# The last wq slabs of a backward pass: requested earlier, into store buffers, and turned in place

## The chip, the cores and the metric

The kernel runs on one core of a Trainium2 chip. The metric is the device time of one execution in microseconds (us), the median of several runs. A profile of one further execution gives the trace; its span is the time from the first to the last instruction of the core.

The engines are named as the profile names them: PE (TensorE, matrix products and transposes), PEld (its weight loads), DVE (VectorE), ACT (ScalarE), POOL (GpSimd, which here copies a little and issues the stores) and SP (SyncE, which here only issues the loads). The loads of SP form the DMA queue q1, the stores of POOL the queue q0. Both are served by the same 16 DMA engines.

## The reference

A decoder step for one token: attention over a cache, a feed-forward layer with squared ReLU, the same attention again and the same feed-forward layer again, with the same weights both times, and the gradients of everything with respect to the inputs (`jax.vjp`). D = 1024, 32 query heads of 128 in 4 groups, a cache of 4 x 65536 x 128 for K and for V, F = 3584, all in bf16.

```python
def _A_ref(x, k_cache, v_cache, wq, wo):
    q = (x @ wq).reshape(B, Sq, Hq, Dh).transpose(0, 2, 1, 3)
    k = jnp.repeat(k_cache, rep, axis=1)
    v = jnp.repeat(v_cache, rep, axis=1)
    scores = jnp.einsum("bhqd,bhkd->bhqk", q, k) * (Dh ** -0.5)
    p = _softmax(scores, axis=-1)
    o = jnp.einsum("bhqk,bhkd->bhqd", p, v)
    return o.transpose(0, 2, 1, 3).reshape(B, Sq, Hq * Dh) @ wo
...
x = x + _A_ref(_layernorm(x), A_k_cache, A_v_cache, A_wq, A_wo)
x = x + _B_ref(_layernorm(x), B_w1, B_b1, B_w2, B_b2)
x = x + _A_ref(_layernorm(x), A_k_cache, A_v_cache, A_wq, A_wo)
x = x + _B_ref(_layernorm(x), B_w1, B_b1, B_w2, B_b2)
```

The outputs are the result and the gradients of x, K, V, wq, wo, w1, b1, w2 and b2.

## The kernel before

**Four passes over the cache.** The K and V caches are read once in each of four passes: the first attention forward, the second forward, the second backward (its dq), and in the last pass (`attn_bwd4`, L1297) dq of the first attention and the K and V gradients of both. Between the passes stand the feed-forward layers. In the code L1 is the first attention layer, L3 the second.

**The arena.** K and V blocks, weight slabs and staged outputs share one buffer in SBUF, `arena`, cut into 20 slots of 128 x 4096 bf16 (1 MB each). A `Slot` (L314) takes a free one, `free` gives it back. In the last pass the slots are of two kinds: those in the set `RING` are meant for stores, the others for loads. `take_one` (L292) gives a caller with `fill=True` the slot of the ring that has been free longest, and any other caller one from outside the ring. When the last group's turn comes, the ring has 11 slots. The kernel only says which slot is used; the waits follow from it: a load into a slot waits until the last reader or the last store of that slot is done.

**The last pass.** It runs over 256 items of 8 columns of 128 positions each, group after group (64 items each), the last group being group 0. Each item goes through the stages in L1484: `vT` turns the V block (8 transposes on PE, L1353, and a copy out of PSUM), `vS` multiplies it with dO, `eT` and `xT` turn the probabilities and their gradients, `dV8` and `dK8` make the output blocks (L1434, copies L161 on ACT or L164 on DVE, store L1440), and `k8` (L1465) multiplies the K block with the gradients for dq. The stages of one item lie some items apart. K and V come in halves of 32 columns, 1 MB each, and one half serves four items. `kv8` (L351) asks for a half at its first use in the program's order, but SP issues requests as soon as the slot is free, so it runs ahead of the engines. SP issues strictly in its own order: a request that waits for its slot holds all behind it. The pass is not ordered by hand; a scheduler arranges each engine's instructions, SP's among them.

**Copies.** `evac` (L150) copies a PSUM tile out, on ACT or DVE, whichever has the smaller planned load; in the last pass bf16 tiles lean to DVE.

**Background work.** `bg` steps other work between the items: outer products for the weight gradients (`g_outer`, `g_outer_wide`, staged in ring slots; stores L1552, L1573), and for each group but the last `g_dn` (L998), which adds that group's part of the gradient `dn1` from two wq slabs by row products on DVE (L595) and sums on ACT (L584).

**The last group's part of dn1.** It needs dq of group 0, known only after the last `k8`, so it is the end of the kernel: `on4` (L1997), called after the last `fold_dq` (L1202). To make it short, wq's slabs for group 0 are loaded and turned ahead. There are two slabs of four row blocks of 128 x 1024 each (L458, 1 MB a slab, runs of 2 KB in DRAM). The class `Rows` (L609) turns them: `tra` (L684) does 8 transposes (L688) and one copy for each of 8 rows of 128 x 1024, `back` (L715) does 8 products with dq for each row (L722), and the sum goes to `dn_finish`. Where `inplace` is not set, `tra` writes the turned row to a view of two further slots (`s_wt`, L619). Then come the layer norm's backward, dx0, and the last outer product `g_outer_last` (L1515).

**When.** The list `end` at L2024 gives functions to be called n items before the end of the pipeline (L871): at 20 the two slabs are requested, into load slots; at 10 `fill4` takes the two `s_wt` slots and turns all eight rows at once, drains the background work and begins `g_outer_last`.

Of the kernel before, what the change touches and what calls it, by code (L numbers as in the profile page):

```python
# [20 lines left out]
def kernel(  # L21
# [31 lines left out]
    R = HQ // G  # L53
    F = B_w1.shape[1]
    DC, FC = D // P, F // P
# [84 lines left out]
    load = {"act": 0.0, "dve": 0.0, "pe": 0.0}  # L140
# [4 lines left out]
    def add_load(act=0.0, dve=0.0, pe=0.0):  # L145
        load["act"] += act
        load["dve"] += dve
        load["pe"] += pe

    def evac(out, in_, kind="bf"):  # L150
        n = 1
        for d in in_.shape[1:]:
            n *= d
        ca = 0.17 + n * 0.00083
        cd = 0.13 + n * (0.00105 if kind == "f32" else 0.00054)

        if PS["pass4"] and kind == "bf":
            ca += 1.5
        if kind == "kta" or kind != "kt" and load["act"] + ca <= load["dve"] + cd:
            load["act"] += 0.17 + n * 0.00083  # L160
            nc.scalar.copy(out=out, in_=in_)  # L161
        else:
            load["dve"] += cd
            nc.vector.tensor_copy(out=out, in_=in_)  # L164
# [119 lines left out]
    def take_pair():  # L284
        both = [(max(FREE[i], FREE[i + 1]), i) for i in range(0, NG, 2) if i in FREE and i + 1 in FREE]
        if not both:
            return None
        i = min(both)[1]
        del FREE[i], FREE[i + 1]
        return i  # L290
# [20 lines left out]
    def odd_one():  # L311
        return any((i ^ 1) not in FREE and t <= NOW["step"] - 16 for i, t in FREE.items())

    class Slot:  # L314
        def __init__(self, name, fill=False, at=None, both=False, load=False):
            self.i = take_one(fill, load) if at is None else at
            self.n = 2 if both else 1
            self.users, self.over = 0, False
            self.t = wide(self.i) if both else GRAN[self.i]
            BUSY.update(range(self.i, self.i + self.n))  # L320
# [87 lines left out]
    B4_LAG = DK_LAG + J // 8  # L408
# [26 lines left out]
    def rows_of(W):  # L435
        return W.rearrange("(kc p) n -> p kc n", p=P)
# [1 line left out]
    def f_rows_of(W):  # L438
        return W.rearrange("(s p j) n -> p s j n", p=P, j=4)

    def slabs(name, load, nk, kper, ncols, ahead=1, flat=False):
        pend = deque()
        ks = deque(range(0, nk, kper))

        def fetch():
            k = ks.popleft()
            i = None
            if ks and flat and NOW["wide"] and not odd_one():
                i = take_pair()
            if i is None:  # L450
                kn = min(kper, nk - k)
                sl = Slot(name)
            else:
                kn = min(2 * kper, nk - k)
                ks.popleft()
                sl = Slot(name, at=i, both=True)
            v = sl.t[:, 0:kn * ncols].rearrange("p (k n) -> p k n", n=ncols)
            nc.sync.dma_start(out=v, in_=load(k, kn))  # L458
            pend.append((k, kn, sl, v))

        def gen():
            while ks or pend:
                while ks and len(pend) < ahead:
                    fetch()
                k, kn, sl, v = pend.popleft()
                for kk in range(kn):
                    NOW["slab"] = sl
                    yield k + kk, v[:, kk, :]
                sl.over = True
                if not sl.users:  # L470
                    sl.free()
        g = gen()
        g_fetch = [fetch for _ in range(ahead)]
        return g, g_fetch

    def prefetch(pair):

        g, fs = pair
        for f in fs:
            f()  # L480
        return g

    def wq_slabs(g, ahead=1):
        v = rows_of(A_wq)
        return slabs("s_wq", lambda k, kn: v[:, k:k + kn, g * 1024:(g + 1) * 1024], DC, 4, 1024, ahead, True)

    def wo_slabs(g, ahead=1):
        v = rows_of(A_wo)
# [120 lines left out]
    class Rows:  # L609
        def __init__(self, pool=None, bufs=NWT):  # L610
            self.pool, self.bufs = pool, bufs
            self.views = deque()
            self.n = 0
            self.made = 0
            self.parts = 0
            if pool is None:

                for _ in range(2):
                    t = Slot("s_wt").t[:, :].rearrange("p (v a b) -> p v a b", v=4, a=8)  # L619
                    self.views.extend(t[:, v, :, :] for v in range(4))  # L620
                self.bufs = 8
            self.queue = deque()
            self.jobs = deque()
            self.feed = None
# [59 lines left out]
        def tra(self, job, kc, slab, q, kind="bf"):  # L684
            k0, w = job["pieces"][q]
            pt = self.ps_wt()
            for i in range(w):
                nc.tensor.transpose(pt[:, i, :], job["cols"](slab, k0 + i), ident_b[:, :])  # L688
            sl = NOW["slab"]
            if job["inplace"]:  # L690
                wt = slab[:, k0 * P:(k0 + w) * P].rearrange("p (a b) -> p a b", b=P)
            elif self.views:
                wt = self.views.popleft()
            else:
                self.made += 1
                if self.made % 2:
                    wt = ktpool.tile([P, 8, P], BF, name="kt", tag="kt")
                else:
                    wt = self.pool.tile([P, 8, P], BF, name="wt", tag="wt", bufs=4)
            evac(wt[:, 0:w, :], pt[:, 0:w, :], kind)  # L700
            add_load(pe=w * 0.1)
            self.queue.append((job, kc, q, wt, sl))
            if job["inplace"]:
                sl.users += 1
            else:
                self.parts += 1
# [59 lines left out]
        def run(self):  # L766
            self.fill()
            first = self.queue[0][0] if self.queue else None
            while first is not None and first["inplace"] and self.queue and self.queue[0][0] is first:
                self.back()  # L770
            self.fill()
            while self.queue:
                self.back()
                self.fill()
# [140 lines left out]
    def gsl(g):  # L915
        return slice(g * R, (g + 1) * R)
# [73 lines left out]
    def dn_finish(dn, first):  # L990
        def fin(y):
            if first:
                nc.vector.tensor_copy(out=dn[:], in_=y)
            else:
                nc.vector.tensor_tensor(out=dn[:], in0=dn[:], in1=y, op=ALU.add)
        return fin

    def g_dn(L, dn, g, first):  # L998
        yield from g_rowdots(wq_slabs(g)[0], DC, L["dqT"][:, gsl(g)], R, dn_finish(dn, first), "%s_dn%d" % (L["name"], g))
# [594 lines left out]
    L1, L3 = new_layer("L1", 0), new_layer("L3", 1)  # L1594
# [31 lines left out]
    lastg = [ITEMS[p][-1][0] for p in range(4)]  # L1626
    firstg = [ITEMS[p][0][0] for p in range(4)]
    PRE = {}

    def pre_load(key, pair):  # L1630
        def f():
            PRE[key] = prefetch(pair())
        return f

    gxbc = bcast_vec(gx[:], DC)
    bg = Background()
# [18 lines left out]
    rows = Rows(DENSE["pool"])  # L1655
# [20 lines left out]
    bg = Background()  # L1676
# [86 lines left out]
    rows = Rows(DENSE["pool"])  # L1763
    wo3b = wo_slabs(firstg[2])
    eps4 = root_ready(L3, lastg[1])
    ahead = [0]
# [75 lines left out]
    bg = Background()  # L1842
# [17 lines left out]
    rows = Rows(DENSE["pool"])  # L1860
# [110 lines left out]
    b4 = ExitStack()  # L1971
    bgpool = b4.enter_context(tc.tile_pool(name="bgpool", bufs=1))
    bg = Background()
# [6 lines left out]
    dn1 = vec.tile([P, DC], F32, name="dn1")  # L1980
# [16 lines left out]
    def on4(g):  # L1997
        if g != lastg[3]:
            bg.add(g_dn(L1, dn1, g, g == firstg[3]))
            bg.normal.append(gwq(g))  # L2000
        else:
            next(PRE["gwq"])
            PRE["rows"].run()
            next(PRE["gwq"])
            dxn1 = ln_bwd(dn1[:], L1["n"], L1["rstd"])
            dx0 = tmp.tile([P, DC], F32, name="dx0")
            nc.vector.tensor_tensor(out=dx0[:], in0=dx1[:], in1=dxn1[:], op=ALU.add)
            col_to_dram(dx0, D, out_1.rearrange("a b d -> (a b d)"))
            run(PRE["gwq"])

    def last_v():

        for g, c8 in ITEMS[3][-3 * J // 8::J // 8]:
            kv8("v", g, c8)

    def fill4():
        PRE["rows"] = Rows()
        PRE["rows"].add(PRE["wq4"], DC, R, lambda: L1["dqT"][:, gsl(lastg[3])], dn_finish(dn1, False))
        PRE["rows"].fill()
        bg.drain()  # L2020
        PRE["gwq"] = g_outer_last(bgpool, out_4, [L3["n"], L1["n"]], [L3["dqT"][:, gsl(lastg[3])], L1["dqT"][:, gsl(lastg[3])]],
                                  lastg[3] * 1024)
        next(PRE["gwq"])
    attn_bwd4(3, L1, L3, on4, bg, b4, [(12 + B4_LAG, last_v), (20, pre_load("wq4", lambda: wq_slabs(lastg[3], 2))), (10, fill4)])  # L2024
    b4.close()
    ps4_stack.close()

# [29 lines left out]
```

## Time and profile before

| | us |
|---|---|
| median of 3 runs | 1936.69 (1935.64 to 1938.51) |
| the profiled execution | 1936.17 |
| its span | 1934.3 |
| mean granted clock of PE | 0.92 |
| PE busy, DVE busy, ACT busy in the span | 1576.4, 1172.2, 1043.8 |
| moved by DMA | 787.62 MB, mean 407 GB/s |
| slab requests of group 0 on SP | 1853.8 and 1855.5 |
| its transposes (L688) | 1903.1 to 1911.7 |
| last `fold_dq` (L1202) | 1915.9 |

All times of the trace are counted from the start of the span. An engine's busy time is the sum of its instructions; the time between an instruction and the one before it is its wait, and the profile names what ended it. For a DMA the trace has the issue (by SP or POOL) and the landing. In the lists of groups, a row gives line, engine, operation, what is written and read, the count, then busy us and mean ns of one, then idle time ahead of it. In the timeline a row gives start, duration, the work, its count and in brackets the wait ahead of it. In the DMA view a queue's row gives packets, MB, and the share of the 16 engines' time.

### The profile page before, as it was taken

What the parts mean: (1) busy time and instruction counts of PE and PEld (TensorE: products, weight loads), DVE (VectorE), ACT (ScalarE), POOL (GpSimd) and SP (SyncE); (2) the same over time, 40 slices, a digit from 0 to 9 for tenths busy, and PEclk for the clock granted to TensorE, in tenths of its full rate; (3) what the DMA queues carried; (4) which work ended last, traced back from release to release, by engine and by line L of the source; (5) the groups of instructions that cost most, each with busy time, mean ns of one, the idle gap of its engine ahead of it and who ended that gap; (6) DMA issues with size and microseconds to landing.
All of it is one profiled execution on the core that took longest, in us unless ns stands there. A gap on an engine that the chain in (4) does not pass through costs nothing. (4 is left out here: it accounts for less than half of the span.)

```text
span 1934.3 us, 66768 instructions
## 1 busy us (share of the span) xinstructions
PE 1576.4 (81%) x30099; PEld 1292.1 (67%) x30099; DVE 1172.2 (61%) x2448; ACT 1043.8 (54%) x1619; POOL 142.4 (7%) x325
## 2 busy tenths in 40 slices
PE   6878778678878878978787878888996987787977
PEld 6878777678777878867677875555654554454544
DVE  5645555255555554645464576777876886676766
ACT  3434334245333535446363465766876785576765
POOL 0000000000000000000000002111211211121211
PEclk9989999799999988998999999898988998798997
DMA  9999999999999999999999997999999999899998
GB/s 393 427 427 424 429 428 416 399 420 412 428 425 428 428 422 330 379 425 429 426 420 426 405 348 298 425 420 387 424 424 413 420 425 423 349 423 397 425 422 321
DMA packets 107148, 787.62 MB, mean 407 GB/s; under 512 B 9440, under 2 KB 16622, under 8 KB 42222
## 3 DMA queue, kind: packets, MB, share of 16 engines
q1 hardware_dynamic: 82782, 617.65, 77.3%
q0 software_dynamic: 24080, 165.70, 20.5%
q8 instruction: 235, 3.85, 0.7%
q14 instruction: 51, 0.42, 0.1%
HBM read 617.62 MB, written 165.69 MB: 405 GB/s over the span
## 5 line engine op out<-in xcount | busy, mean ns | idle before, releaser
L164 DVE COPY kt<-ps_tr 128x1024 bf16<-128x1024 bf16 x736 | 505.8, 688 | 427.1 <-PE ps_tr L1030 239.5
L161 ACT CAST arena<-ps_gg 128x1024 bf16<-128x1024 f32 x457 | 444.2, 1011 | 183.2 <-PE ps_gg L1434 132.4
L1030 PE MATMUL ps_tr<-ident_b,arena 128*128 128x128 bf16 x3840 | 308.4, 225 | 48.0 <-DMA arena<-in_A_k_cache_dram 35.3
L161 ACT COPY kt<-ps_tr 128x1024 bf16<-128x1024 bf16 x180 | 188.6, 1054 | 184.5 <-PE ps_tr L1224 107.2
L164 DVE CAST arena<-ps_gg 128x1024 bf16<-128x1024 f32 (+2 forms) x186 | 222.4, 1196 | 80.1 <-PE ps_gg L1434 36.0
L1030 PEld LDWEIGHTS <-arena 128*128 128x128 bf16 x3840 | 231.8, 101 | 56.7 <-DMA arena<-in_A_k_cache_dram 37.8
L1434 PE MATMUL ps_gg<-GG,xt 64*128 64x512 bf16 x1024 | 209.8, 408 | 51.2 <-DVE arena L164 36.7
L1131 PE MATMUL ps_acc<-arena 128*128 128x64 bf16 (+4 forms) x4096 | 204.6, 197 | 46.1 <-DMA arena<-in_A_v_cache_dram 33.7
L1048 PE MATMUL ps_sc<-L_qpad,kt 128*128 128x64 bf16 (+7 forms) x3584 | 182.6, 194 | 23.1 <-issue 11.7
L1353 PE MATMUL ps_tr<-ident_b,arena 128*128 128x128 bf16 x1824 | 178.1, 232 | 28.5 <-DMA arena<-in_A_v_cache_dram 25.7
L1113 ACT ACTIVATE arena<-S_sb,L_negm 128x128 bf16<-128x128 f32 x256 | 165.3, 1006 | 57.2 <-DVE L_negm L1098 43.6
L1224 PE MATMUL ps_tr<-ident_b,arena 128*128 128x128 bf16 x2032 | 161.7, 224 | 40.6 <-DMA arena<-in_A_v_cache_dram 39.1
L1131 PEld LDWEIGHTS <-arena 128*128 128x128 bf16 x4096 | 160.0, 101 | 52.1 <-DMA arena<-in_A_v_cache_dram 37.7
L1353 PEld LDWEIGHTS <-arena 128*128 128x128 bf16 x1824 | 117.6, 103 | 84.7 <-issue 54.2
L1048 PEld LDWEIGHTS <-kt 128*128 128x128 bf16 x3584 | 152.0, 100 | 27.3 <-issue 12.8
L1224 PEld LDWEIGHTS <-arena 128*128 128x128 bf16 x2032 | 122.6, 100 | 46.0 <-DMA arena<-in_A_v_cache_dram 41.7
L1465 PEld LDWEIGHTS <-arena 128*128 128x128 bf16 x2048 | 92.4, 101 | 56.4 <-issue 38.5
L1434 PEld LDWEIGHTS <-xt 64*128 64x128 bf16 x1024 | 64.4, 94 | 97.8 <-issue 60.2
L1113 ACT ACTIVATION_READ_ACCUMULATOR arena<-S_sb,L_negm 128x1 f32 x256 | 128.2, 501 | 0.0
L584 ACT ACTIVATE mv_t<-mv_t 128x1024 bf16<-128x1024 bf16 x96 | 102.0, 1064 | 43.0 <-DVE mv_t L595 42.8
L1278 PE MATMUL ps_acc<-dsT,arena 128*128 128x64 bf16 (+7 forms) x2048 | 102.4, 194 | 12.4 <-DMA arena<-in_A_k_cache_dram 7.2
L1390 PE MATMUL ps_sc<-DOB,kt 128*128 128x64 bf16 (+3 forms) x1824 | 112.3, 197 | 0.1
(319 smaller groups left out, 2104.3 us busy)
## 6 DMA issues: line engine op xcount, KB each, us to landing
arena<-in_A_k_cache_dram SPq DMA_DIRECT2D x82, 2048.0 KB, 21.3
arena<-in_A_v_cache_dram SPq DMA_DIRECT2D x79, 2048.0 KB, 20.1
out_dram<-arena POOLq DMA_DIRECT2D x149, 1024.0 KB, 15.6
arena<-in_A_v_cache_dram SPq DMA_DIRECT2D x84, 1024.0 KB, 13.1
arena<-in_A_k_cache_dram SPq DMA_DIRECT2D x84, 1024.0 KB, 14.6
arena<-in_A_wo_dram SPq DMA_DIRECT2D x22, 1024.0 KB, 14.9
arena<-in_B_w_dram SPq DMA_DIRECT2D x21, 1024.0 KB, 10.0
arena<-in_A_wq_dram SPq DMA_DIRECT2D x18, 1024.0 KB, 13.4
```

Of the source, the lines that this page charges most:

```text
L161: nc.scalar.copy(out=out, in_=in_)
L164: nc.vector.tensor_copy(out=out, in_=in_)
L584: nc.scalar.activation(out=t[:, :], in_=t[:, :], func=ACTF.Copy, accum_out=y[:, kc:kc + 1])
L1030: nc.tensor.transpose(pt[:, i, :], kb8[:, i, :], ident_b[:, :])
L1048: nc.tensor.matmul(state["ps_s"][:, s:s + w, :].rearrange("p a b -> p (a b)"), lhsT=kt[:, i, :], rhs=L["qpad"][:, g, 0:w, :].rearrange("p ...
L1113: nc.scalar.activation(out=E(p, g, c0, SU)[:, :, h], in_=S[:, h, :], func=ACTF.Exp, bias=L["negm"][:, g, su, h:h + 1], scale=SCALE, accum_ ...
L1131: nc.tensor.matmul(ps_o[:, 0:w, :], lhsT=vb8[:, i, :], rhs=E(p, g, c, w), start=(c % SU == 0), stop=(c % SU == SU - 1), skip_group_check=True)
L1224: nc.tensor.transpose(pt[:, i, :], vb8[:, i, :], ident_b[:, :])
L1278: nc.tensor.matmul(ps_dq[:, 0:w, :].rearrange("p a b -> p (a b)"), lhsT=kb8[:, i, :], rhs=dsT[:, s:s + w, :].rearrange("p a b -> p (a b)") ...
L1353: nc.tensor.transpose(pt[:, i, :], vb8[:, i, :], ident_b[:, :])
L1390: nc.tensor.matmul(state["ps_dp"][:, s:s + w, :].rearrange("p a b -> p (a b)"), lhsT=vt[:, i, :], rhs=DOB[:, g, 0:w, :].rearrange("p a b - ...
L1434: nc.tensor.matmul(pg[:, 512 * h:512 * h + 512], lhsT=xt[64 * h:64 * h + 64, j1 // 8 + m, :], rhs=gg[64 * h:64 * h + 64, :, :].rearrange(" ...
```

## The change

The two slabs are requested 48 and 38 items before the end instead of both at 20, and into ring slots (`fill=True` by the new argument `ring`). From item -28 on, every second item turns one row (`last_turn`), in place: the copy goes back into the slab's own slot. The two `s_wt` slots and the code for them go. At item -10 `fill4` no longer turns rows; at the end `on4` runs the same products by `begin` and `back`.

```diff
-    def slabs(name, load, nk, kper, ncols, ahead=1, flat=False):
+    def slabs(name, load, nk, kper, ncols, ahead=1, flat=False, ring=False):
...
-                sl = Slot(name)
+                sl = Slot(name, ring)
...
-    def wq_slabs(g, ahead=1):
+    def wq_slabs(g, ahead=1, ring=False):
         v = rows_of(A_wq)
-        return slabs("s_wq", lambda k, kn: v[:, k:k + kn, g * 1024:(g + 1) * 1024], DC, 4, 1024, ahead, True)
+        return slabs("s_wq", lambda k, kn: v[:, k:k + kn, g * 1024:(g + 1) * 1024], DC, 4, 1024, ahead, True, ring)
...
-            self.views = deque()
...
-            if pool is None:
-
-                for _ in range(2):
-                    t = Slot("s_wt").t[:, :].rearrange("p (v a b) -> p v a b", v=4, a=8)
-                    self.views.extend(t[:, v, :, :] for v in range(4))
-                self.bufs = 8
...
-            elif self.views:
-                wt = self.views.popleft()
...
             next(PRE["gwq"])
-            PRE["rows"].run()
+            last_rows.begin(last_job)
+            while last_rows.queue:
+                last_rows.back()
             next(PRE["gwq"])
...
+    last_wq, last_fetch = wq_slabs(lastg[3], 2, True)
+    last_rows = Rows()
+    last_job = last_rows.job(DC, R, lambda: L1["dqT"][:, gsl(lastg[3])], dn_finish(dn1, False))
+    last_job["inplace"] = True
+
+    def last_turn():
+        kc, slab = next(last_wq)
+        run(last_rows.front(last_job, kc, slab))
+
     def fill4():
-        PRE["rows"] = Rows()
-        PRE["rows"].add(PRE["wq4"], DC, R, lambda: L1["dqT"][:, gsl(lastg[3])], dn_finish(dn1, False))
-        PRE["rows"].fill()
+        next(last_wq, None)
         bg.drain()
...
-    attn_bwd4(3, L1, L3, on4, bg, b4, [(12 + B4_LAG, last_v), (20, pre_load("wq4", lambda: wq_slabs(lastg[3], 2))), (10, fill4)])
+    tail = [(48, last_fetch[0]), (38, last_fetch[1])] + [(28 - 2 * k, last_turn) for k in range(DC)] + [(10, fill4)]
+    attn_bwd4(3, L1, L3, on4, bg, b4, [(12 + B4_LAG, last_v)] + tail)
```

In the built programs the arithmetic is the same, instruction for instruction in kind and number, but for the choice between ACT and DVE for one copy. SP's order differs at these places only: the first slab now stands right behind the second slab of group 1's `g_dn` (requested at 1750.06 in the trace of before) and takes a slot whose last store is the one issued at 1750.58; the V half that was requested at 1754.96 stands two places later, behind the K half of 1756.93 and the V half of 1774.18; the second slab stands between the V half of 1792.36 and the K half of 1801.30 and takes a slot whose last store is the one issued at 1792.92; and the two slabs at 1853.79 and 1855.49 are gone. The 64 transposes of the rows are spread over what was 1847 to 1897.

## Prediction

> **What bounds the kernel now.** I read the slices of the page first, then the windows of the last 160 us, then the waits there, then SP's requests and the landing times of its transfers.
>
> ```profile
> DMA  9999999999999999999999997999999999899998
> HBM read 617.62 MB, written 165.69 MB: 405 GB/s over the span
> ```
>
> The DMA engines are full nearly everywhere, and the change moves no byte more or less. So it can only matter where it opens or closes a gap. This window table shows the end of the last pass (busy us and count of PE, PEld, DVE, ACT, POOL, then granted clock, DMA share, GB/s):
>
> ```profile
> 1875.60:1885.00 9.40, 0.03 (x2) 0.00 (x0) 0.33 (x5) 1.20 (x2) 0.53 (x1) 0.76 1.02 427
> 1885.00:1897.50 12.50, 12.42 (x105) 7.00 (x105) 6.92 (x9) 5.63 (x6) 0.53 (x1) 0.50 0.96 401
> ...
> 1860.00:1872.40 12.40, 12.17 (x169) 7.74 (x169) 10.16 (x18) 10.01 (x12) 2.98 (x5) 1.00 1.03 421
> 1902.00:1916.00 14.00, 12.90 (x200) 9.08 (x199) 11.43 (x19) 11.15 (x13) 1.26 (x2) 1.00 1.00 386
> ```
>
> TensorE is the pacing engine (12.17 of 12.4 us busy) until it stands still at 1875.6. Behind that it runs 12.5 us at clock 0.50. The PE timeline names what it waited for there, and at one earlier place:
>
> ```profile
> 1885.08 0.34 PE L1465 MATMUL ps_acc<-X,arena 128*128 128x64 bf16 x3 [9.45 <-DMA arena<-in_A_k_cache_dram]
> ```
>
> ```profile
> 1804.76 0.23 PE L1353 MATMUL ps_tr<-ident_b,arena 128*128 128x128 bf16 x1 [1.84 <-DMA arena<-in_A_v_cache_dram]
> ```
>
> Both are reads. Which half a request brings, and when TensorE first uses it, I took from the order of the built program laid beside the trace. These are SP's requests ahead of the large wait, and those at the places where the changed program's order puts the two slabs:
>
> ```profile
> 1853.79 2.08 SPq L458 DMA_DIRECT2D arena<-in_A_wq_dram  x2
> 1864.37 1.30 SPq L361 DMA_DIRECT2D arena<-in_A_k_cache_dram  x2
> ```
>
> ```profile
> 1750.06 0.38 SPq L458 DMA_DIRECT2D arena<-in_A_wq_dram  x1
> 1754.96 0.33 SPq L361 DMA_DIRECT2D arena<-in_A_v_cache_dram  x1
> 1756.93 0.33 SPq L361 DMA_DIRECT2D arena<-in_A_k_cache_dram  x1
> ```
>
> ```profile
> 1792.36 0.43 SPq L361 DMA_DIRECT2D arena<-in_A_v_cache_dram  x1
> 1801.30 0.33 SPq L361 DMA_DIRECT2D arena<-in_A_k_cache_dram  x1
> 1801.77 0.40 SPq L361 DMA_DIRECT2D arena<-in_A_v_cache_dram  x1
> ```
>
> Last, what the read queue (q1) gets beside the store queue (q0), in 1757 to 1766 with a wq slab at its head, then in 1795 to 1815 with K and V halves alone:
>
> ```profile
> q0 software_dynamic: 403, 2.92, 77.3%
> q1 hardware_dynamic: 397, 0.85, 24.1%
> ```
>
> ```profile
> q1 hardware_dynamic: 621, 4.53, 53.7%
> q0 software_dynamic: 613, 3.92, 46.9%
> ```
>
> Packets are shared about one for one (397 to 403). A wq row is 2 KB and a store's run 8 KB, so a slab (1.05 MB) takes 1.05/(0.85/9) = 11.1 us to pass, a K or V half 1.05/(4.53/20) = 4.6 us. With stores absent (1768.2 to 1772: 1.49 MB in 3.8 us) a slab takes 2.7 us. The Trainium skill ("DMA: Bandwidth & Descriptors", Queues, rings and completion order) says each engine takes turns between its queues by packets; with one 2 KB row against one 8 KB run that gives q1 a fifth of 424 GB/s, an estimate of 12.4 us for a slab, and would add 1.3 us to the sum.
>
> **Part 1, the slabs leave 1853.8 and 1855.5.** Two slow slabs stood ahead of the K halves there. In the changed order the next K halves stand behind the same TensorE counts, so they are asked for at these times, not at 1864.4 and 1865.3. The K half at 1844.19 landed at 1859.6, so they land near 1864 and 1869, 11 us or more before their use at 1875.6 and some 10 us later. The wait of 9.45 us goes. So does the half clock: 105 instructions at the rate of 1860 to 1872.4 (169 in 12.4) take 7.7 us, not 12.5, a gain of 4.8. Sum -14.2. Bounds: -9.5 (the clock falls for some other wait) to -14.2. Next due are the last two K halves; their buffers come free with the same TensorE counts as the halves at 1864, so they too come 30 us earlier than at 1898.
>
> **Part 2, the 64 transposes and 8 copies.**
>
> ```profile
> L688 PE MATMUL ps_tr<-ident_b,arena 128*128 128x128 bf16 x64 | 5.0, 220 | 0.0
> ```
>
> They leave 1903.1 to 1911.7, where PE is 12.90 of 14 us busy, and go to what is now 1847 to 1897, where it is 12.17 of 12.4. PE paces both, so 5.0 us leave and 5.0 come: 0. Bounds: -5.0 if the waits of the new place hide them, +1.1 (the 14 - 12.90 idle at the old one). The copies (six on DVE at 686 ns, two on ACT at 1015 ns, 6.1 us) find 2.2 us free on each engine in every 12.4: hidden.
>
> **Part 3, buffers.** Two buffers for turned rows are no longer taken at item -10; nothing read into that range waits for them. But stores go round 9 buffers, not 11. 18 large stores in 1802 to 1875 are one per 4.06 us: a buffer comes back after 36.5 us in place of 44.6. A store lands 23.2 us after issue (median there), and filling takes about 10 us (four quarters over four items of 2.5 us). 3 us are left: 0. Bounds 0 to +5.
>
> **Part 4, the first slab.** Its buffer was last emptied by the store issued at 1750.58, which took 17.0 us; SP stands until 1767.6 with everything behind it. Behind it are the K half of 1756.93 (used at 1779.6) and the V halves of 1774.18 and 1754.96, in this order. At 1767.6 the store queue runs empty, so the slab passes in 2.7 us, in the place of the V half; K lands just in time. The V half now comes between the V half of 1774.18 and the K half of 1779.8, and every later read lands a half later: 4.6 us, plus some tenths for the late start: 5. The V half of 1790.68 landed at 1804.7, when PE had waited 1.84 us already, so all of it is new wait. Bounds: 0 (1773 to 1782 moved only 2.61 MB, room for one more half) to 7.
>
> **Part 5, the second slab.** It stands between the requests of 1792.36 and 1801.30 and waits for the store issued at 1792.92, 13.1 us, until 1806.0. The K half behind it needs a buffer that part 4 moves from 1801.3 to 1806.3, so SP loses nothing. Then it takes 11.1 us of the read queue. The V half of 1801.77 landed 21.2 us later, at 1823.0, and its transposes began at 1824.74: 1.7 us to spare. New wait 9.4; but TensorE standing still makes no stores, and the two halves behind the slab go faster as the stores run out (from 4.6 us each toward 2.7): I take 2 off, 7.4. Bounds: 1.0 (2.7 - 1.7) to 9.4. What comes next had 6 us or more to spare and shifts with PE.
>
> **Part 6, the clock.** The wait of 1.84 us was followed by 3.4 us at 0.50 and the one of 9.45 by 12.5. Two new waits of 7 us cost 0.5 to 4.8 each by these; I take 2.5 for both. The Trainium skill ("TensorE: Matmul & The Clock Gate", Why this matters for your kernels) sets the limit at gaps of about 3 us; the wait of 1.84 shows the trace less patient, and by the rule both new waits would still cost.
>
> Sum: -14.2 + 0 + 0 + 5 + 7.4 + 2.5 = +0.7. The profiled execution took 1936.17 us (span 1934.3, 1.9 around it), 0.5 below the median of the runs. 1936.2 + 0.7 = 1936.9, by the median 1937.4: I say **1937.5**. From the last group's dq (1915.9) to the end nothing changes.
>
> **Rivals.**
> - *Faster: the reads are not held.* The room of 1773 to 1782 takes the V half (0) and the second slab meets a nearly empty store queue (1.0 to 3, say 2), with 1 for the clock: -14.2 + 3 = -11.2, 1926. For it: the 290 GB/s there, and stores that thin out as soon as PE waits. Against it: q0 was never empty in 1795 to 1815.
> - *Slower: the second slab at the head of the read queue.* Place: 1816 to 1830, ahead of the K and V halves of 1801.3 and 1801.77. Price: 9.4 in full, part 4 at 7, and half clock as after 1885 for one wait and 2 for the other (6.8): 23.2 - 14.2 = +9.0, 1945. It decides once both waits together, clock included, pass 14.2 us. For it: the V halves asked for at 1774.18, 1790.68 and 1801.77 had 0, 0 and 1.7 us to spare, while the reads of 1843.21 and 1844.19, the last ahead of the slabs' old place, had 31 and 6. Against it: the relief by idle stores.
> - *Store buffers:* the old wait goes, but copies wait for one of 9 buffers: +5, 1942. Against it: 3 us of room, and a shorter store backlog after an early wait.
>
> **Chances.** Forecast 0.40, faster rival 0.25, second slab 0.28, store buffers 0.07. A change under 0.2% (3.9 us) can't be told from none here. The forecast's own range is 1933 to 1942; it gives 0.05 faster, 0.28 same, 0.07 slower. The first rival gives 0.22 faster and 0.03 same, the others 0.03 same and 0.32 slower. Together 0.27, 0.34, 0.39. Range 1928 to 1945.
>
> **What would show it.** In the new profile: no wait of TensorE for K near 1875 to 1890, and clock 1.0 there (part 1); L688 spread before the end (part 2); a wait of L1353 for V of some 7 us near 1803 to 1810 (part 4) and of L1465 or L1353 of some 7 near 1829 to 1837 (part 5), each with half clock behind it; no copy waiting for a store (part 3). I am wrong if the two early waits stay under 8 us together or pass 18, or if a K wait remains at the end.

## The result, and the profile after

The changed kernel takes 1942.16 us, the median of 18 runs (1936.24 to 1946.80). The kernel before, run beside it, takes 1936.83 (18 runs, 1929.03 to 1942.41). The ratio is 1.003, with a 95% interval from 1.0018 to 1.0042: the change costs about 5 us. A later repetition (below) gave 1.0031, from 1.0017 to 1.0044.

The profiled execution of the changed kernel took 1936.24 us and was the fastest of its 18. When TensorE resumes after a long wait for DVE (1773.00 us before, 1769.57 after) it was already 3.4 us ahead. About 1 us of that was there at SP's last request ahead of the places where the orders differ (1750.06 before, 1749.06 after). The rest came while the slab of that request landed, in 20.9 us before and 18.5 after; in the profile of the repetition, with the changed order too, it landed in 21.5, so I take the lead for chance. The change's first own request is made at 1764.31. So I compare the stretches behind that point, not the spans: 161.3 us from there to the end before, 164.8 after, and 167.6 in the profile of the repetition (1771.7 to 1939.3).

First three of the windows that the prediction showed of the kernel before, and one for a new slow stretch; the window table's columns are as explained there.

```profile
1875.60:1885.00 9.40, 8.77 (x130) 5.88 (x128) 6.98 (x14) 7.06 (x9) 1.98 (x4) 1.00 1.01 421
1885.00:1897.50 12.50, 11.98 (x167) 7.88 (x166) 10.61 (x22) 10.00 (x12) 2.12 (x4) 1.00 0.99 412
1827.20:1840.80 13.60, 8.22 (x72) 4.71 (x72) 3.21 (x5) 4.56 (x5) 1.27 (x2) 0.50 1.01 426
1902.00:1916.00 14.00, 11.68 (x193) 7.87 (x190) 10.92 (x24) 9.73 (x12) 1.80 (x3) 1.00 0.64 264
```

The standstill at 1875.6 to 1885 is gone (8.77 of 9.4 us busy, clock 1.00), as part 1 said. In its place stands half clock from 1827.2 to 1840.8. And in 1902 to 1916 TensorE is less busy than before (11.68 us, not 12.90), with the DMA engines at 0.64, not full.

The PE timeline, at its three long waits behind 1800:

```profile
1804.03 0.29 PE L1344 MATMUL ps_tr<-ident_b,arena 128*128 128x128 bf16 x1 [2.61 <-DMA arena<-in_A_v_cache_dram]
...
1828.88 0.23 PE L1456 MATMUL ps_acc<-X,arena 128*128 128x64 bf16 x1 [4.38 <-DMA arena<-in_A_k_cache_dram]
...
1833.84 0.40 PE L1344 MATMUL ps_tr<-ident_b,arena 128*128 128x128 bf16 x2 [3.70 <-DMA arena<-in_A_v_cache_dram]
```

The first is the V half of part 4, the two others are the halves behind the second slab, of part 5. SP's requests in the changed kernel:

```profile
1764.31 0.38 SPq L458 DMA_DIRECT2D arena<-in_A_wq_dram  x1
1764.78 0.46 SPq L361 DMA_DIRECT2D arena<-in_A_k_cache_dram  x1
1770.75 1.14 SPq L361 DMA_DIRECT2D arena<-in_A_v_cache_dram  x2
...
1803.96 0.38 SPq L458 DMA_DIRECT2D arena<-in_A_wq_dram  x1
1804.44 0.61 SPq L361 DMA_DIRECT2D arena<-in_A_k_cache_dram  x1
1805.10 0.48 SPq L361 DMA_DIRECT2D arena<-in_A_v_cache_dram  x1
```

The first slab was held for its buffer until 1764.31 and the second until 1803.96, each with K and V behind it. While the second passes, from 1810 to 1822, the two queues show nearly the shares that part 5 had taken from 1757 to 1766:

```profile
q0 software_dynamic: 498, 3.68, 73.2%
q1 hardware_dynamic: 552, 1.32, 27.8%
```

552 packets to 498, but 1.32 MB to 3.68: the read queue brings 1.32 MB in 12 us. The second slab landed 20.1 us after its request, at 1824.0, and the V half ahead of it at 1812.9: 11.1 us to pass, as part 5 had it.

The 64 transposes of the rows, in the list of groups by tile for 1840 to 1905 (ns min/median/max, then first and last start):

```profile
L681 PE MATMUL ps_tr<-ident_b,arena x64: 219/219/230, 1856.3 to 1898.2; 128*128 128x128 bf16 x64
```

They are spread over 42 us, as the change says. The chain of waits at the end of the pass shows what paces there now:

```profile
1903.08 1.02 ACT arena L161
...
1904.14 0.42 PE ps_gg L1503 x2
...
1904.59 1.02 ACT arena L161
...
1905.65 0.41 PE ps_gg L1425 x2
...
1906.08 1.02 ACT arena L161
...
1907.15 0.42 PE ps_gg L1503 x2
...
1907.59 1.02 ACT arena L161
```

ACT copies a product tile out of PSUM in 1.02 us, TensorE fills the next in 0.42, and so on, some 1.5 us a round: from 1903 to 1909 the chain runs through ACT's copies, and TensorE fits its other products in between. (Left out are pieces of 0.02 to 0.04 us, the time to issue.) So TensorE's own work doesn't set the pace there alone.

Stretch by stretch, in us, with what the prediction's parts give for the same stretch:

| from ... to | before | after | difference | predicted |
|---|---|---|---|---|
| TensorE resumes ... first transpose of the late V half (1804.76, 1804.03) | 31.8 | 34.5 | +2.7 | +5 (part 4) |
| ... first transposes of the V half asked for at 1801.77, in the changed kernel at 1805.10 | 20.0 | 29.8 | +9.8 | +9.9 (parts 5 and 6) |
| ... where TensorE comes to the K half that it waited for before (1875.6, 1890.5) | 50.9 | 56.7 | +5.8 | +5.0 (part 2, the transposes come) |
| ... the end | 58.7 | 43.9 | -14.8 | -19.2 (parts 1 and 2, the transposes leave) |
| sum | 161.3 | 164.8 | +3.5 | +0.7 |

The three costs together came as predicted to within 2 us. What lacks is in the last row: 4.4 us of the gain. The third row holds more than transposes, since half clock goes on to 1840.8; what the transposes alone cost there is read below, from the same stretches of three placings.

### The profile page after: what moved, and what is told of

Its sections match the earlier page's. It is cut to its first block, busy times and chain, and to the rows that moved or that the text cites. A ratio compares the mean times of both kernels' runs of the same rounds, so it can differ in the third digit from the quotient of the medians.

```text
span 1934.4 us, 66781 instructions
## 1 busy us (share of the span) xinstructions
PE 1594.3 (82%) x30099; PEld 1302.7 (67%) x30099; DVE 1171.7 (61%) x2447; ACT 1045.3 (54%) x1620; POOL 142.1 (7%) x325
## 5 line engine op out<-in xcount | busy, mean ns | idle before, releaser
L1425 PE MATMUL ps_gg<-GG,xt 64*128 64x512 bf16 x1024 | 215.4, 417 | 38.2 <-DVE arena L164 23.2
L1425 PEld LDWEIGHTS <-xt 64*128 64x128 bf16 x1024 | 63.5, 94 | 86.0 <-issue 49.3
## 6 DMA issues: line engine op xcount, KB each, us to landing
arena<-in_A_wq_dram SPq DMA_DIRECT2D x18, 1024.0 KB, 13.6
```

Of the source, the lines that this page charges most:

```text
L1425: nc.tensor.matmul(pg[:, 512 * h:512 * h + 512], lhsT=xt[64 * h:64 * h + 64, j1 // 8 + m, :], rhs=gg[64 * h:64 * h + 64, :, :].rearrange(" ...
```

## The experiments

Each was timed beside the kernel before: 1936.51 us in the first group of four, 1936.43 in the second, 1938.28 in the third. So the ratio to it counts; a difference of medians from two groups is rough.

**Turning late.** All eight rows are turned at item -10 as before; the requests and the buffers stay as changed.

```diff
-    tail = [(48, last_fetch[0]), (38, last_fetch[1])] + [(28 - 2 * k, last_turn) for k in range(DC)] + [(10, fill4)]
+    tail = [(48, last_fetch[0]), (38, last_fetch[1])] + [(10, last_turn)] * DC + [(10, fill4)]
```

> Requests as in the changed kernel (48 and 38), all eight rows turned in place at item -10. Theory (the end of the pass is paced by copies out of PSUM, so the 5.0 us of transposes had mostly been free there, while at their new place they cost 5 to 6 us): about 4 us faster than the changed kernel, 1938 us. Rival (as predicted, 5 us leave and 5 come): as the changed kernel, 1942 us.

Measured: 1937.4 us, ratio 0.9997 (0.9986 to 1.0008). The waits for reads are much the same as in the changed kernel (3.09, 3.92 and 3.66 us, there 2.61, 4.38 and 3.70). The medians differ by 4.8 us from the changed kernel's. So the place of the transposes is worth most of the loss, and part 2's zero is wrong.

**The second slab late.** The first slab keeps its place and its store buffer, with four rows turned early. The second is requested at -20 into a load buffer, its four rows turned at -10.

```diff
-                sl = Slot(name, ring)
+                sl = Slot(name, ring and k == 0)
...
-    last_wq, last_fetch = wq_slabs(lastg[3], 2, True)
+    last_wq, last_fetch = wq_slabs(lastg[3], 1, True)
...
-    tail = [(48, last_fetch[0]), (38, last_fetch[1])] + [(28 - 2 * k, last_turn) for k in range(DC)] + [(10, fill4)]
+    tail = [(48, last_fetch[0]), (20, last_fetch[0])] + [(28 - 2 * k, last_turn) for k in range(4)] + [(10, last_turn)] * 4 + [(10, fill4)]
```

> First slab at 48 into a store buffer and its four rows from -28 on; second slab at 20 into a load slot as before, its four rows at -10. Theory (the second slab at -38 is what holds the reads at 1829 to 1838 and costs some 8 us of waits and 13.7 us of half clock): these waits are gone, the K wait of 9.45 us at the end falls under 4 us since one slow slab stands there and not two: 1930 to 1933 us, faster than both kernels. Rival (the turning in place or the fewer store buffers cost the time): 1940 us or more.

Measured: 1933.13 us, ratio 0.9984 (0.9970 to 0.9999), below both kernels. One wait of TensorE above 0.9 us is left behind 1800, the V half of part 4:

```profile
1805.86 0.29 PE L1344 MATMUL ps_tr<-ident_b,arena 128*128 128x128 bf16 x1 [3.75 <-DMA arena<-in_A_v_cache_dram]
```

Neither the waits near 1829 to 1838 nor one at 1885 are there. One slow slab at the old place is borne, two were not; and the second slab's new place, with its store buffer, is what cost the 9.8 us in the table's second row, which is 1.0 here (21.0 us against 20.0).

**Both at -48.** The second request is made with the first.

```diff
-    tail = [(48, last_fetch[0]), (38, last_fetch[1])] + [(28 - 2 * k, last_turn) for k in range(DC)] + [(10, fill4)]
+    tail = [(48, last_fetch[0]), (48, last_fetch[1])] + [(28 - 2 * k, last_turn) for k in range(DC)] + [(10, fill4)]
```

> Both slabs requested at item -48, rows as in the changed kernel. Theory (what a slab costs depends on what it meets: behind the wait of 1758 to 1770 the store queue is empty, so a slab passes in 3 us, not 11): the waits of 8 us at 1829 to 1838 go, up to 5 us of V waits between 1775 and 1805 come: 1934 to 1938 us. Rival (every early slab costs the same wherever it stands): 1942 us.

Measured: 1939.08 us, ratio 1.0008 (0.9997 to 1.0018): between the two times that were named. It didn't get the place it was meant for: SP's order put a V half between the slabs, the second was requested at 1779.04, and from 1779 to 1790 the stores had 52.6% of the DMA time again. Three waits for reads were left behind 1800, of 3.95, 1.09 and 4.05 us.

**Long runs.** The second request brings 1 MB of the K cache, in runs of 8 KB, into the same buffer at the same place. Half of the last group's part of the x gradient is then formed from other data.

```diff
-            nc.sync.dma_start(out=v, in_=load(k, kn))
+            if ring and k:
+                nc.sync.dma_start(out=sl.t[:, :].rearrange("p (j d) -> p j d", d=DH), in_=half(KVIN["k"], 0, 0))
+            else:
+                nc.sync.dma_start(out=v, in_=load(k, kn))
```

> The changed kernel, but the second request brings 1 MB of the K cache in runs of 8 KB in place of the second wq slab with runs of 2 KB, at the same place in SP's order (half of the last group's part of the x gradient is then computed from other data). Theory (the slab is slow because packets are shared one for one with the stores' 8 KB): it passes in 4.6 us, not 11, the waits at 1829 to 1838 fall from 8 to about 2 us: 1935 us. Rival (SP standing still for the store's landing delays the reads): as the changed kernel, 1942 us.

Measured: 1935.21 us, ratio 0.9992 (0.9979 to 1.0005), 7 us below the changed kernel with the same bytes. The DMA queues from 1810 to 1822 (packets, MB, share):

```profile
q1 hardware_dynamic: 380, 2.76, 54.6%
q0 software_dynamic: 381, 2.34, 46.8%
```

One packet each again (380 to 381), but now 2.76 MB of reads in 12 us where it was 1.32. Of the two waits near 1829 to 1838 one of 2.44 us is left. By these counts it is the runs' length that makes a slab slow beside stores. The Trainium skill ("DMA: Bandwidth & Descriptors", Queues, rings and completion order) says that each DMA engine goes round its queues by packets, and the traces agree in both cases: 552 to 498 with 2 KB rows, 380 to 381 with 8 KB runs.

**The second slab late, all rows late.** The two findings joined: the second slab as above, all eight rows turned at -10.

```diff
-    tail = [(48, last_fetch[0]), (20, last_fetch[0])] + [(28 - 2 * k, last_turn) for k in range(4)] + [(10, last_turn)] * 4 + [(10, fill4)]
+    tail = [(48, last_fetch[0]), (20, last_fetch[0])] + [(10, last_turn)] * DC + [(10, fill4)]
```

(The line taken out is that of the second experiment.)

> The first slab stays at -48 in a store buffer, the second is requested at -20 into a load buffer, and all eight rows are turned at -10. If the two costs found so far (the second slab's place, the early turning) are separate, the four rows that were still turned early give their half of about 5 us: 1930 to 1931. If early turning costs only because it falls into the stretch that the second slab had delayed, turning late gains nothing more here: 1933. If the turning at the end now lies on the path, with the last dq some 12 us earlier than before: 1936.

Measured: 1932.78 us, ratio 0.9981 (0.9968 to 0.9994). The four rows give nothing more (0.35 us). That is not because they were free: the third stretch of the table takes 53.5 us with four rows turned early and 50.7 here, but the last takes 48.4 and 51.0. From TensorE's resumption to the end both profiles take the same, 157.3 and 157.2 us. So the gains don't add, and something else sets the end; the next run shows what.

**The kernel before with long runs.** Both late requests of the kernel before bring 1 MB of the K cache each, in runs of 8 KB. The last group's part of the x gradient is formed from other data.

```diff
-            nc.sync.dma_start(out=v, in_=load(k, kn))
+            if long:
+                nc.sync.dma_start(out=sl.t[:, :].rearrange("p (j d) -> p j d", d=DH), in_=half(KVIN["k"], 0, k // 4))
+            else:
+                nc.sync.dma_start(out=v, in_=load(k, kn))
...
```

(The other lines hand `long=True` to the two late requests.)

> The kernel before, with the two late requests bringing 1 MB each of the K cache in runs of 8 KB (the last group's part of the x gradient is then formed from other data). If the wait of 9.45 us came from two slabs of 2 KB rows at some 11 us each, they now pass in some 4.6 each, the K halves behind them land some 13 us earlier, and the wait and its half clock go: 1922 to 1926 if all of it is gained, 1928 to 1932 if the end of the pass is set by the copies of the last gradient products out of PSUM, which take part of it back. If the K halves were late for want of a free buffer: 1936, with the wait still there.

Measured: 1931.9 us, ratio 0.9981 (0.9970 to 0.9992). The wait of 9.45 us and its half clock are gone, no wait above 0.9 us is left behind 1807, the last dq comes 12.5 us earlier (done at 1903.6, before at 1916.1), and the time falls by 4.5 us only. The window table of the kernel before, for the last 40 us:

```profile
1895.00:1905.00 10.00, 9.65 (x125) 5.74 (x122) 6.82 (x14) 7.30 (x8) 1.28 (x2) 0.87 0.89 318
1905.00:1915.00 10.00, 9.52 (x155) 6.83 (x152) 7.87 (x13) 8.04 (x11) 1.26 (x2) 1.00 1.00 406
1915.00:1925.00 10.00, 7.91 (x104) 4.07 (x101) 7.64 (x21) 5.68 (x7) 1.99 (x4) 0.82 0.70 288
1925.00:1935.00 10.00, 1.23 (x4) 0.22 (x3) 1.23 (x1) 1.99 (x3) 2.53 (x4) 0.50 0.43 174
```

and of this one:

```profile
1895.00:1905.00 10.00, 8.96 (x156) 6.34 (x153) 7.76 (x17) 7.78 (x10) 1.27 (x2) 1.00 1.01 420
1905.00:1915.00 10.00, 7.22 (x76) 3.17 (x74) 6.49 (x15) 5.81 (x6) 2.84 (x5) 0.71 1.02 423
1915.00:1925.00 10.00, 0.00 (x0) 0.00 (x0) 0.00 (x0) 0.20 (x1) 1.12 (x2) 0.50 0.90 371
1925.00:1935.00 10.00, 0.00 (x0) 0.00 (x0) 0.00 (x0) 0.00 (x0) 0.00 (x0) 0.53 0.03 13
```

The DMA share (the number before the last) was 0.89, 1.00, 0.70 and 0.43 in the last four windows before. Here it is 1.01, 1.02, 0.90 and 0.03: TensorE has ended by 1915, and the stores are still draining. The chain of waits says the same:

```profile
1893.59 0.51 issue
1894.10 22.51 DMA out_dram<-arena
1916.61 0.02 issue
```

Its largest piece is a store that takes 22.51 us to land, beside DMA engines at 1.01 and 1.02. The last store, issued at 1917.2, takes 11.8 us to land, where the last of the kernel before took 3.0. The time is within the 1928 to 1932 that was named for the case that the copies take part of the gain back, but the number came out right for the wrong reason: the DMA engines took it.

**Nine store buffers.** The kernel before, with two store buffers taken out of use.

```diff
+[(48, lambda: Slot("hold", True)), (38, lambda: Slot("hold", True)),
```

(put at the head of its list of calls)

> The kernel before, with two store buffers taken out of use from -48 and -38 on, and nothing else changed. If nine buffers are enough: 1936 to 1938. If copies wait for a store's buffer: 1941 or more, with waits of ACT or DVE for a DMA in the last 120 us.

Measured: 1936.4 us, ratio 0.9998 (0.9988 to 1.0008). Two copies did wait for a store's buffer, one on ACT (2.15 us) and one on DVE (2.24), TensorE waited 2.24 us behind them at 1870.30, and its wait for K became 1.65 us shorter (7.80, not 9.45). Timeline, ACT and PE:

```profile
1869.23 1.01 ACT L161 CAST arena<-ps_gg 128x1024 bf16<-128x1024 f32 x1 [2.15 <-DMA out_dram<-arena]
...
1887.02 0.29 PE L1465 MATMUL ps_acc<-X,arena 128*128 128x64 bf16 x2 [7.80 <-DMA arena<-in_A_k_cache_dram]
```

Part 3's zero holds for the time, though its 3 us were not always left.

**Without turning.** The changed kernel without the 64 transposes and the 8 copies: the products take the slabs as they lie, so the last group's part of the x gradient is another.

```diff
-            pt = self.ps_wt()
-            for i in range(w):
-                nc.tensor.transpose(pt[:, i, :], job["cols"](slab, k0 + i), ident_b[:, :])
+            asis = job.get("asis")
+            if not asis:
+                pt = self.ps_wt()
+                for i in range(w):
+                    nc.tensor.transpose(pt[:, i, :], job["cols"](slab, k0 + i), ident_b[:, :])
...
-            evac(wt[:, 0:w, :], pt[:, 0:w, :], kind)
-            add_load(pe=w * 0.1)
+            if not asis:
+                evac(wt[:, 0:w, :], pt[:, 0:w, :], kind)
+                add_load(pe=w * 0.1)
...
-    last_job["inplace"] = True
+    last_job["inplace"] = last_job["asis"] = True
```

> The changed kernel without the 64 transposes and 8 copies of the last rows (the products take the slabs as they lie, so the last group's part of the x gradient is wrong). If the transposes cost their 5 us of TensorE where they now stand: 1936 to 1938. If they lie beside its waits there: 1942.

Measured: 1940.32 us, ratio 1.0021 (1.0010 to 1.0032). Beside the changed kernel (1942.16, another group) that is only 1.8 us less, and it lies 2.9 above the kernel that turns late and does more. So the three kernels were timed once more, beside each other.

**Three placings of the turning, in one group.**

> The changed kernel as it is, on the chip and in the hour of the two runs beside it: 1942, from 18 runs. If its own spread had made it look slower: 1938 to 1939.

> The kernel that turns all rows at -10, a second time: 1937.4 before. If the transposes cost 5 us where the change put them and nothing at the end: 1937, and the kernel without turning the same. If the earlier difference was between jobs: equal to the changed kernel within 2 us.

> The changed kernel without turning, a second time: 1940.3 before, which is 2.9 above the kernel that turns late though it does less. If that was chance: 1937 to 1938. If it stays at 1940 or above, turning late itself helps, and what it shifts has to be found in the order of the copies.

Measured: turned early (the changed kernel) 1942.6, ratio 1.0031 (1.0017 to 1.0044); turned late 1939.28, 1.0013 (1.0004 to 1.0023); not turned 1938.56, 1.0007 (0.9999 to 1.0016). The order of the last two is now the other way round and their intervals overlap: turning at the end costs between nothing and 1 us. Turning early costs 4.0 us beside not turning and 3.3 beside turning late (1.8 and 4.8 between the groups before). The same stretches in the two profiles of each kernel show where, with the last one parted at the group's last dq (us):

| rows turned | third row | TensorE at the K half ... last dq | last dq ... the end |
|---|---|---|---|
| kernel before (with its K wait) | 50.9 | 40.5 | 18.2 |
| early | 56.7, 56.9 | 22.8, 22.7 | 21.0, 23.0 |
| at -10 | 52.8, 52.4 | 27.0, 27.0 | 18.1, 17.7 |
| not | 52.4, 52.5 | 22.8, 22.8 | 22.8, 22.9 |

At their new place the transposes cost 3.9 to 4.5 us. When they leave the old one, the last dq does come 4.2 us sooner, but what follows takes 3 to 5 us longer, so that the end stays where it was. Behind the last dq TensorE now has 10 of the output products of L1425 to do (in the kernel before and with the rows turned at -10 it has 2), and ACT and DVE have 13 or 14 copies into the arena and not 11. The windows near the end show this work (the three traces are some microseconds apart). Turned early:

```profile
1912.00:1916.00 4.00, 3.03 (x57) 2.22 (x57) 2.27 (x7) 3.08 (x4) 0.66 (x1) 0.98 0.47 197
1916.00:1920.00 4.00, 3.50 (x33) 1.73 (x32) 2.46 (x8) 2.02 (x2) 0.61 (x2) 0.50 0.66 266
```

turned late:

```profile
1912.00:1916.00 4.00, 3.94 (x49) 2.72 (x49) 3.92 (x5) 2.92 (x4) 0.53 (x1) 1.00 0.90 376
1916.00:1920.00 4.00, 3.98 (x67) 2.92 (x67) 2.82 (x7) 4.00 (x6) 0.72 (x1) 1.00 0.44 179
```

not turned:

```profile
1912.00:1916.00 4.00, 3.04 (x33) 1.79 (x34) 2.80 (x10) 2.27 (x3) 0.58 (x2) 0.52 0.66 269
1916.00:1920.00 4.00, 3.87 (x53) 2.22 (x49) 1.83 (x2) 2.02 (x2) 0.58 (x2) 0.62 0.63 267
```

The clock (the third number from the end) stays at 1.00 with the transposes there, and falls to 0.50 to 0.62 without them. Without them TensorE has gaps of 0.4 to 1.0 us each ahead of the last products, in which it waits for copies; with them they are 0.41 at most up to the last dq. Of six profiles with no transposes there (those of both slabs at -48 and of long runs among them), five fell to half clock between 0.8 us ahead of the last dq and 1.7 behind it; in the eight with transposes there the clock falls 5.3 to 8.4 us behind it. The sixth is the first profile of the changed kernel, which keeps 1.00 until 9.4 us behind, is the fastest run of that kernel, and has the shortest way from the last dq to the end among the six (21.0 us). It has waits of 0.65 and 0.73 us at the same place all the same, so gaps of that size don't bring the fall each time, and what decides it isn't shown.

**A quarter of each slab.** The kernel before, with 128 rows of 2 KB a request in place of 512. The last group's part of the x gradient is formed from a quarter of the slab.

```diff
-            nc.sync.dma_start(out=v, in_=load(k, kn))
+            if quarter:
+                v = v[:, 0:1, :]
+                nc.sync.dma_start(out=v, in_=load(k, 1))
+            else:
+                nc.sync.dma_start(out=v, in_=load(k, kn))
...
-                    yield k + kk, v[:, kk, :]
+                    yield k + kk, v[:, 0 if quarter else kk, :]
...
```

(The other lines hand `quarter=True` to the two late requests.)

> The kernel before with late requests of 128 rows of 2 KB in place of 512, so 1.57 MB less to read in all, 3.8 us of the DMA engines at some 418 GB/s (the last group's part of the x gradient is then formed from a quarter of the slab). The wait for K near 1885 goes, as it did with long runs, where the median was 1931.9 and the DMA engines stayed full up to 1918. If the end is set by what the DMA engines still have to move, the time comes out those 3.8 us below: 1928. If TensorE and the copies set it: 1932, as with long runs. If the halves were late for another reason than the slabs: 1936.

Measured: 1929.97 us (five runs), ratio 0.9958 (0.9945 to 0.9971). Each beside its own kernel before, long runs gained 4.5 us and this one 8.3, so 3.8 more, for the same work of the engines and 1.57 MB less; 3.8 was expected if DMA sets the end. (The two differences are from two groups; the ratios give 4.5.) Its windows:

```profile
1905.00:1915.00 10.00, 6.16 (x58) 2.53 (x56) 6.29 (x14) 5.26 (x6) 3.64 (x6) 0.73 1.01 421
1915.00:1925.00 10.00, 0.00 (x0) 0.00 (x0) 0.00 (x0) 0.00 (x0) 0.32 (x1) 0.50 0.61 248
```

TensorE does as much as with long runs. Counted from where it resumes, its last product ends 1.3 us earlier than there, but the last store lands 4.5 us earlier, and the whole takes 153.2 us where the three profiles without a late K wait and with all bytes take 157.2 to 157.8 (the two with the second slab late, and long runs). So once the waits are gone, the DMA engines set the end.

## Why the prediction came out as it did

The time of the changed kernel was put at 1937.5 us with 1928 to 1945 for the range, and came out at 1942.16: inside, 4.7 us above. The likeliest case was "no change"; what came is a loss of 0.3%, a little over what can be told from none. The chances had slower first (0.39), but neither of the two rivals on that side is what happened. That the time is inside is owed in part to the range's width and to luck: by the table, part 4 cost 2.3 us less than its term while the last row gained 4.4 less, and these partly cancel.

- **What bounds the kernel.** The prediction showed the DMA engines full, said that the change can only matter where it opens or closes a gap in them, and then reckoned with TensorE alone. Both views are needed. TensorE's waits say where time is lost; what closing a wait is worth is capped by the idle time of the DMA engines that is left behind it, with the same bytes to move. The last 40 us of the kernel before were shown with the long runs; these are the same windows of the changed kernel:

```profile
1895.00:1905.00 10.00, 9.28 (x145) 6.28 (x141) 7.62 (x16) 7.70 (x10) 1.80 (x3) 1.00 0.90 369
1905.00:1915.00 10.00, 7.97 (x127) 5.15 (x125) 7.44 (x17) 6.72 (x8) 1.25 (x2) 1.00 0.50 206
1915.00:1925.00 10.00, 7.68 (x90) 3.87 (x89) 7.21 (x16) 6.07 (x6) 2.13 (x4) 0.89 0.73 299
1925.00:1935.00 10.00, 1.23 (x4) 0.22 (x3) 1.04 (x1) 2.03 (x3) 2.38 (x4) 0.50 0.43 174
```

Ten times one less each share, the idle time is 9.8 us before (1.1, 0, 3.0, 5.7) and 14.4 here (1.0, 5.0, 2.7, 5.7): 4.6 more, with the stretch of these two profiles 3.5 us longer. That is the loss seen from the DMA engines, not its cause: here they wait for work. Of the 9.8 us before, 4.0 can't be used, as the last store lands at 1931.0, the span ends at 1934.3 and the last window goes on to 1935. So 5.8 was the most that closing the wait at 1885 could bring, and part 1 booked 14.2.

- **Part 1, -14.2.** The wait and its half clock went. With the rows turned at -10, so that the last stretch holds the same work as before, it is 13.6 and 14.0 us shorter: in the changed kernel the size was right. As a property of the slabs it was too large: with them made fast in the kernel before, that stretch became 3.2 us shorter and the time 4.5, as the DMA engines were full to 1915. The later TensorE comes to the stretch, the more of the 14.2 it gets: 3.2 us with no delay, 7.7 with 3.6 and 10.3 with 6.3 (the two versions with the second slab late), 14.0 with 14.0 (rows late). In the changed kernel the earlier stretches had put it some 18 us behind (the first three rows of the table).
- **Part 2, 0.** This is the step that failed, and with it the sentence that from the last group's dq to the end nothing changes. The transposes cost 3.9 to 4.5 us where they were put, by the stretches (by the medians 1.8 to 4.8, in four comparisons). Where they had been, TensorE did pace up to the last dq, as was read from its 12.90 of 14 us busy: without them the dq comes 4.2 us sooner. But output products and their copies fall behind the dq instead, the rest takes 3 to 5 us longer, and at the end about nothing comes back: 43.9 and 45.8 us for the last stretch, against 45.1 and 44.7 with the transposes in it. That these products go at the pace of ACT's copies of 1.02 us, and not of TensorE, is how the chain reads; the fall of the clock adds to it (21.0 us from dq to the end in the profile without it, 22.0 to 23.0 in the five with it). Neither was tried alone. The bound of +1.1 was TensorE's idle time at the old place and left out what stands behind the dq.
- **Part 3, 0.** Right in time (nine buffers: 1936.4), with one wait of TensorE of 2.24 us, of which the later K wait took up 1.65. In the changed kernel's profile no copy waits for a store.
- **Part 4, +5.** Right in mechanism, smaller in size: +2.7, inside its bounds of 0 to 7. The wait at 1804.03 was 2.61 us where some 7 had been named, and 2.64 in the repetition: 0.8 more than before. Another, of 1.19 us for K at 1789.65 (1.19 in the repetition too), had not been foreseen.
- **Parts 5 and 6, +7.4 and +2.5.** Together 9.8 by the table. The place, the cause and the price were right: the two waits are 4.38 and 3.70 us, 8.1 in all, at 1828.9 and 1833.8, where 1829 to 1837 had been named; the queue shares repeat; long runs take most of it away. The half clock was longer than taken: 13.6 us, of which TensorE worked 8.22, so some 4 us lost where 2.5 stood (an estimate, half of 8.22), and part of it falls into the third row: without transposes that row is still 1.5 us longer than before.
- **Signs.** No wait for K at the end, L681 spread, the two early waits together 10.7 us, between the 8 and 18 that had been set as limits, no copy waiting for a store: as said, but for the V wait of 2.61 us in place of some 7. And yet the time was 4.7 us off, since none of the signs was about what stands behind the last dq. "From the last group's dq to the end nothing changes" was wrong as well: 18.2 us before (1916.1 to 1934.3), 21.0 after (1913.3 to 1934.4), 23.0 in the repetition.
- **Rivals.** "Reads are not held" fell with the waits. "The second slab at the head of the queue" had the mechanism, which is part 5's too; its 9.4 us was above the 8.1 of the two waits (part 5 had 7.4), and its sum of +9.0 above the loss. "Store buffers" fell: no copy waited for one.

What stays open: whether ACT's copies alone set the pace behind the last dq, what brings the clock's fall there, and why part 4's wait is shorter than the half that was put in front of it.

## What to carry to other kernels

Before a wait is booked as a gain, add up the idle time of the DMA engines from it to the end, without what lies behind the last landing: with the bytes unchanged and the engines at the same rate, closing it can't give more than that. Work that is moved out of the last microseconds can bring one result sooner and leave the end where it was: count what then falls behind that result, and look in the chain for two engines that alternate, not at busy shares alone. Two loads with short runs beside a full store queue are better placed far apart: the version with one slab at -48 and one at -20, turned at -10 (1932.78 us, ratio 0.9981), is 0.2% faster than the kernel before.

## What the hardware showed that was not expected

The clock fell to half with no wait of 1 us ahead of it. In the repetition of the changed kernel it falls at 1915.84, and TensorE's longest wait since 1840 is one of 0.65 us for DVE, which ends there; without turning it falls at 1912.17, behind waits of 0.45 and 0.41 us, and one of 0.96 comes after. The Trainium skill ("TensorE: Matmul & The Clock Gate", Why this matters for your kernels) names idle gaps above about 3 us as what brings the half rate back; by that rule none of these would have. But the first profile of the changed kernel has waits of 0.65 and 0.73 us at the same place and stays at 1.00, so the short gaps alone don't decide it.

At about one packet a turn, 2 KB rows beside 8 KB store runs got 1.32 of 5.0 MB in 12 us, and 8 KB runs at the same place 2.76 of 5.1: the bytes that a load gets depend on the runs of the other queue as much as on its own.
